# Three small token slots of a routed mixture of experts, moved from a split-weight path of their own into column tiles between the half layers of other experts

## The chip, the cores and the metric

The kernel runs on one core of one Trainium2 chip. The metric is the device time of one execution in microseconds (us); several runs are taken and their median is compared. Beside it there is one profiled execution, with a trace of every instruction on each engine: TensorE's matmuls (PE), its weight loads (PEld), VectorE (DVE), ScalarE (ACT), GpSimd (POOL) and SyncE (SP). The suffix q marks an engine's own queue work: DMA issues, register loads, waits.

## What is computed

A masked attention over 8 batches and 8 heads of 576 positions gives 4608 token rows of 512 numbers. Each row goes to the one of eight experts with the largest gate logit, through two matrix products with a ReLU between them, and is scaled by its gate weight:

```python
logits = x @ w_gate                       # (4608, 512) @ (512, 8)
expert_idx = np.argmax(logits, axis=1)
for e in range(8):
    mask = expert_idx == e
    h = np.maximum(x[mask] @ w1[e], 0.0)  # (512, 1024)
    out[mask] = gate_w[mask, None] * (h @ w2[e])  # (1024, 512)
```

The reference, run on its own inputs, sends 591, 497, 610, 490, 661, 437, 657 and 665 rows to experts 0 to 7.

## The kernel before

Attention and routing fill the first 240 us or so. The rest is the expert stage, with some expert work (`fillers`, then `base(0)`) already mixed into the end of the first part.

An expert's first 512 tokens are a base window (`base`, `window`, L255 to L306). Of experts 0, 2, 4 and 6 the first 256 are done early by `fillers`, so that their later windows have 256 tokens; those of 1, 3, 5 and 7 have 512. Tokens beyond 512 lie in slots of 128 (`slot`, L872). With the counts above that is 1, 0, 1, 0, 2, 0, 2 and 2 slots, eight in all, and `RSLOT = 8` of them are laid out statically. A loop at the end of the program, of `nslots - RSLOT` turns, takes what is beyond that number; here it has none.

Weights arrive in four chunks of 1 MB per expert (`wcat`; 80 such loads, issued by SP), each with a quarter of w1 and of w2. `wsplit` (L209) divides each chunk into a high part `whi` (ACT, L212) and a low part `wlo` (DVE, L213) in the fast fp32r format, and each product is taken as three matmuls: high by high, high by low, low by high. Raw and split weights have four buffers each in the expert stage.

A window goes by half layers: one chunk has two, a window eight. A half layer is twelve matmuls of w1 into bank `t` (L287 to L289), a ReLU on ACT (`hh`, L292), the low part on DVE (`hl`, L293), and then, one half layer late (`pend`), twelve (for 256 tokens six) matmuls of w2 (L276 to L278). A slot has four chunks of twelve matmuls of 256 columns (L892 to L894), two transposes (L904), and six matmuls of 512 columns (L911 to L913); four transposes of its tokens (L879) come first. Token rows are fetched by GpSimd (`gather`, L227) and written back by it (`finish`, L242).

The order is a list of jobs (L942): windows of experts 1 to 7 with one slot after each, and the last slot behind that: b1 s0 b2 s1 b3 s2 b4 s3 b5 s4 b6 s5 b7 s6 s7. While one job runs, the next one's gather and transposes are issued: gather before the first step, transposes at steps 0 and 2 (`PRE`). Base windows and slots share two PSUM banks named `v` for transposes. `slot_tables` (L654) computes, on DVE, which tokens lie in which slot, during the early windows.

A program orders the instructions of each engine by priority, which is program order except where the kernel raises it (`tc.high_priority`); an engine then works through its list in that order.

Of the kernel before, what the change touches and what calls it, by code (L numbers as in the profile page):

```python
# [7 lines left out]
F32 = mybir.dt.float32  # L8
# [27 lines left out]
RSLOT = 8  # L36
MAXSLOT = 40
XW = DM + 16
NCH = 4
CW = DF // NCH  # L40
CHW = 2 * 1024
LAG_T = 3
# [68 lines left out]
def host_constants(np):  # L111
    f = np.float32
    c = {}
    m = np.full((128, 3, 64), NEG, f)
    for p in range(128):
        q = p % QB
        m[p, 0, q + 1:q + QB + 1] = 0.0
        m[p, 1, max(q + 1, QB if p < 2 * QB else 0):q + QB + 1] = 0.0
        r, a = divmod(p % 64, SR)
        if r < 3:  # L120
            m[p, 2, r * SR:r * SR + a + 1] = 0.0
        else:
# [6 lines left out]
    parts = [tri, rows * np.arange(128, dtype=f),  # L129
             rows * np.arange(E, 0, -1, dtype=f), rows * np.arange(NT, dtype=f),  # L130
             np.arange(128, dtype=f).reshape(128, 1), np.arange(1, 129, dtype=f).reshape(128, 1)]
    c["blob"] = np.concatenate(parts, axis=1)
    return c
# [3 lines left out]
def moe_attn(ctx, tc, qk, vv, wg, wcat, blob0, blob, out):  # L137
# [29 lines left out]
    pid_sb = cst[:, 256 + E + NT:258 + E + NT]  # L167
    identb = const.tile([128, 128], BF16, name="identb")
# [4 lines left out]
    sidacc = const.tile([128, 2, MAXSLOT], F32, name="sidacc")  # L173
# [14 lines left out]
    srow = const.tile([128, MAXSLOT], I32, name="srow")  # L188
# [66 lines left out]
    def window(e, idc, odc, gpool, xpool, ypool, rows=N + 1):  # L255
# [4 lines left out]
        xh = xpool.tile([128, 4, n], F32R, name=f"xh{nt}")  # L260
        xl = xpool.tile([128, 4, n], F32R, name=f"xl{nt}")
# [42 lines left out]
    def base(e, gpool, xpool, ypool):  # L304
        tr = range(2 if e in EXP else 0, 4)
        return window(e, [ids[:, t, e:e + 1] for t in tr], [oids[:, t, e:e + 1] for t in tr], gpool, xpool, ypool)  # L306

    with ExitStack() as actx:
# [323 lines left out]
        def fillers():  # L632
            def make(e):
                w = window(e, [eids[:, t, e:e + 1] for t in range(2)], [eoids[:, t, e:e + 1] for t in range(2)], xge, xep, yep,
                           1 + EG * GT * 128)
                next(w)
                return w
# [15 lines left out]

        def slot_tables():  # L654
# [9 lines left out]
            cum = rte  # L664
            for sh in (1, 2, 4):
                nx = rt.tile([128, E], F32, name=f"cum{sh}")
                nc.vector.tensor_copy(out=nx[:, 0:sh], in_=cum[:, 0:sh])
                nc.vector.tensor_tensor(out=nx[:, sh:E], in0=cum[:, sh:E], in1=cum[:, 0:E - sh], op=ALU.add)
                cum = nx
# [7 lines left out]
            nc.vector.tensor_copy(out=srow, in_=es)  # L677
# [6 lines left out]
            nc.vector.tensor_tensor(out=oe, in0=oe, in1=first.unsqueeze(1).broadcast_to([128, NT, E]), op=ALU.mult)  # L684
            key = rt.tile([128, NT], F32, name="skey")
            nc.vector.tensor_reduce(out=key, in_=oe, axis=AX.X, op=ALU.add)
# [4 lines left out]
            nc.vector.scalar_tensor_tensor(out=key, in0=t1, scalar=1.0, in1=key, op0=ALU.is_ge, op1=ALU.mult)  # L691
            for g in range(NG):
# [5 lines left out]
                bm = scratch(GT * MAXSLOT).rearrange("p (t k) -> p t k", k=MAXSLOT)  # L698
                nc.vector.tensor_tensor(out=bm, in0=iota_sb[:, 1:MAXSLOT + 1].unsqueeze(1).broadcast_to([128, GT, MAXSLOT]),
                                        in1=key[:, gs].unsqueeze(2).broadcast_to([128, GT, MAXSLOT]), op=ALU.is_equal)  # L700
                bb = scratch(GT * MAXSLOT).bitcast(BF16).rearrange("p (t a k) -> p t a k", a=2, k=MAXSLOT)
                nc.vector.tensor_tensor(out=bb[:, :, 0, :], in0=bm, in1=tokhi_sb[:, gs].unsqueeze(2).broadcast_to([128, GT, MAXSLOT]),
# [4 lines left out]
                for c in range(GT):  # L707
                    nc.tensor.matmul(sb[:, 0:2 * MAXSLOT], am[:, c, :], bb[:, c, :, :].rearrange("p a k -> p (a k)"),
                                     start=(c == 0), stop=(c == GT - 1))
                acc = sidacc.rearrange("p a k -> p (a k)")  # L710
                nc.vector.tensor_tensor(out=acc, in0=sb[:, 0:2 * MAXSLOT], in1=acc, op=ALU.add)
            hi_ = rt.tile([128, MAXSLOT], F32, name="shi_")
            nc.vector.scalar_tensor_tensor(out=hi_, in0=sidacc[:, 0, :], scalar=128.0, in1=sidacc[:, 1, :], op0=ALU.mult, op1=ALU.add)
            nc.vector.tensor_copy(out=sids, in_=hi_)
            out_index(souts, hi_)
# [132 lines left out]
        with tc.high_priority():  # L848
            make_ids()
            cur = base(0, xge, xep, yep)  # L850
            next(cur)
# [75 lines left out]

    def row_load(in_tensor, engines):
# [12 lines left out]

    jobs = []  # L942
    for e in range(1, E):
        jobs.append(lambda e=e: base(e, xgm, xtm, yp))
        if e >= 1:
            jobs.append(lambda s=e - 1: static_slot(s))
    for s in range(E - 1, RSLOT):
        jobs.append(lambda s=s: static_slot(s))
# [135 lines left out]
```

## Time and profile before

| | us |
|---|---|
| median of three runs | 691.72 (690.84 to 693.19) |
| the profiled execution's own time | 688.08 |
| its span, first to last instruction | 686.2 |
| TensorE matmul busy | 648.9 (95% of the span) |
| TensorE weight load busy | 542.4 (79%) |
| VectorE busy | 431.2 (63%) |
| ScalarE busy | 354.5 (52%) |
| bytes moved | 149.85 MB, 218 GB/s over the span |

Matmuls are pipelined: a record's duration is its latency, and two neighbours overlap. What one costs in a dense stretch is the distance from its start to the next start, and that is read from the timeline. A stretch is one between two starts of the same kind of work.

### The profile page before, as it was taken

The numbers are of one execution on the slowest core, as the hardware profiler recorded it, in microseconds if no ns is written. First come the engines' busy times: TensorE is split into PE (matmuls) and PEld (weight loads), VectorE is DVE, ScalarE is ACT, GpSimd is POOL, SyncE is SP. The second block draws the span as 40 slices with busy tenths as digits, with TensorE's granted clock in tenths as the row PEclk, the third lists the DMA queues.
The fourth block names the chain that finished last, engine by engine and source line by source line (L and its number), as shares of the span: only waits on it lengthen the run. The fifth ranks groups of instructions, "written<-read, shape, count | busy, mean of one in ns | idle before, by whom it ended". The sixth has DMA issues, their size and how long they took to land.

```text
span 686.2 us, 14770 instructions
## 1 busy us (share of the span) xinstructions
PE 648.9 (95%) x5996; PEld 542.4 (79%) x5996; DVE 431.2 (63%) x796; ACT 354.5 (52%) x617; POOL 150.7 (22%) x168
## 2 busy tenths in 40 slices
PE   4999999799889899999999999999999999999997
PEld 3876768587778688897888988878888878988885
DVE  5667878567835579796336775346675248683364
ACT  1556666565555544564337574246473247572362
POOL 3222223511321302053005132022032041100021
PEclk9899999999999999999999999999999999999999
DMA  9879998985645657469327867337675257664140
GB/s 281 244 225 262 331 307 247 349 300 169 217 176 206 240 187 251 159 238 342 140 92 266 296 245 261 118 124 262 261 257 208 107 191 264 258 218 170 66 180 21
DMA packets 36695, 149.85 MB, mean 218 GB/s; under 512 B 5261, under 2 KB 5645, under 8 KB 26384
## 3 DMA queue, kind: packets, MB, share of 16 engines
q1 hardware_dynamic: 24576, 118.50, 51.1%
q0 software_dynamic: 6432, 20.26, 8.1%
q10 hardware_dynamic: 5616, 10.12, 4.1%
q8 instruction: 48, 0.79, 0.5%
q14 instruction: 23, 0.19, 0.1%
HBM read 129.69 MB, written 20.22 MB: 218 GB/s over the span
## 4 chain that ended last, share of the span: by engine, by line
PE 74%; issue 12%; DVE 5%; ACT 4%; DMA 2%; POOL 1%; POOLq 1%; SPq 0%; another core or an unknown queue 0%
PE t L287 8%; PE t L289 8%; PE t L288 8%; PE y L276 6%; PE y L278 6%; PE y L277 6%; PE s L399 4%; PE t L441 2%; PE s L412 2%; PE v L455 2%; PE v L466 2%; PE s L276 2%; PE s L278 2%; PE s L277 2%; PE v L265 2%
## 5 line engine op out<-in xcount | busy, mean ns | idle before, releaser
L213 DVE TENSOR_TENSOR wlo<-raw,whi 128x1024 fp32r<-128x1024 f32 x160 | 192.7, 1222 | 86.9 <-ACT whi L212 75.6
L212 ACT CAST whi<-raw 128x1024 fp32r<-128x1024 f32 x160 | 163.2, 1050 | 67.1 <-PE s L278 26.1
L287 PE MATMUL t<-xh,whi 128*128 128x256 f32 (+1 forms) x384 | 125.2, 327 | 1.9 <-ACT xh L221 1.3
L288 PE MATMUL t<-xl,whi 128*128 128x256 f32 (+1 forms) x384 | 123.8, 323 | 0.3 <-DVE xl L222 0.3
L289 PE MATMUL t<-xh,wlo 128*128 128x256 f32 (+1 forms) x384 | 123.4, 322 | 0.1
L292 ACT ACTIVATE hh<-t 128x256 fp32r<-128x256 f32 (+1 forms) x96 | 43.5, 453 | 115.1 <-PE t L289 109.2
L293 DVE SCALAR_TENSOR_TENSOR hl<-t,hh 128x256 fp32r<-128x256 f32 (+1 forms) x96 | 49.0, 510 | 75.6 <-ACT hh L292 75.2
L287 PEld LDWEIGHTS t<-xh,whi 128*128 128x128 f32 x384 | 72.4, 189 | 9.8 <-ACT xh L221 1.8
L288 PEld LDWEIGHTS t<-xl,whi 128*128 128x128 f32 x384 | 72.6, 189 | 7.2 <-DVE xl L222 0.7
L289 PEld LDWEIGHTS t<-xh,wlo 128*128 128x128 f32 x384 | 72.5, 189 | 6.4 <-DVE wlo L213 0.9
L276 PE MATMUL y<-whi,hh 128*128 128x512 f32 x192 | 76.2, 397 | 0.0
L277 PE MATMUL y<-wlo,hh 128*128 128x512 f32 x192 | 75.0, 391 | 0.0
L278 PE MATMUL y<-whi,hl 128*128 128x512 f32 x192 | 75.0, 396 | 0.0
L248 POOL DMA_INDIRECT out_dram<-y,oids x24 | 26.9, 1121 | 215.1 <-DVE y L247 166.5
L350 POOL TENSOR_TENSOR prob<-prob,ri 128x512 f32<-128x512 f32 x40 | 42.5, 1062 | 121.8 <-DVE ri L349 94.1
L155 ACT COPY xT<-v 128x270 f32<-128x270 f32 (+1 forms) x80 | 30.0, 481 | 29.0 <-PE v L455 13.0
L278 PEld LDWEIGHTS y<-whi,hl 128*128 128x128 f32 x192 | 35.6, 188 | 8.3
L276 PEld LDWEIGHTS y<-whi,hh 128*128 128x128 f32 x192 | 36.0, 188 | 6.7 <-ACT hh L292 0.7
L277 PEld LDWEIGHTS y<-wlo,hh 128*128 128x128 f32 x192 | 36.1, 188 | 5.7
L346 DVE TENSOR_REDUCE sm<-prob 128x8 f32<-128x512 f32 x40 | 27.3, 683 | 20.6 <-ACT prob L344 20.4
L340 DVE TENSOR_REDUCE nm<-s 128x8 f32<-128x512 f32 x40 | 27.3, 683 | 18.8 <-PE s L399 14.2
L344 ACT ACTIVATE prob<-prob 128x512 f32<-128x512 f32 x40 | 25.2, 631 | 22.9 <-DVE prob L343 22.1
(173 smaller groups left out, 1167.2 us busy)
## 6 DMA issues: line engine op xcount, KB each, us to landing
raw<-in_wcat_dram SPq DMA_DIRECT2D x80, 1024.0 KB, 6.5
xd<-xr ACTq DMA_DIRECT2D x36, 264.0 KB, 4.8
vl<-in_vv_dram SPq DMA_DIRECT2D x16, 512.0 KB, 6.5
qkl<-in_qk_dram SPq DMA_DIRECT2D x16, 264.0 KB, 3.8
vt<-in_vv_dram SPq DMA_DIRECT2D x16, 256.0 KB, 4.7
qk<-in_qk_dram SPq DMA_DIRECT2D x8, 484.0 KB, 5.5
qk<-in_qk_dram SPq DMA_DIRECT2D x8, 432.0 KB, 4.9
qk<-in_qk_dram SPq DMA_DIRECT2D x8, 396.0 KB, 6.3
```

Source lines behind the costliest of these rows:

```text
L155: nc.scalar.copy(out=out, in_=in_)
L212: nc.scalar.copy(out=hi[:, sl], in_=raw[:, sl])
L213: i = nc.vector.tensor_tensor(out=lo[:, sl], in0=raw[:, sl], in1=hi[:, sl].bitcast(F32), op=ALU.subtract)
L276: nc.tensor.matmul(yb[t], hh[:, ts], whi[:, w], start=(j == 0), stop=False)
L277: nc.tensor.matmul(yb[t], hh[:, ts], wlo[:, w], start=False, stop=False)
L278: nc.tensor.matmul(yb[t], hl[:, ts], whi[:, w], start=False, stop=(j == 7))
L287: nc.tensor.matmul(hb[:, 0:n], whi[:, w], xh[:, dc, :], start=(dc == 0), stop=False)
L288: nc.tensor.matmul(hb[:, 0:n], whi[:, w], xl[:, dc, :], start=False, stop=False)
L289: nc.tensor.matmul(hb[:, 0:n], wlo[:, w], xh[:, dc, :], start=False, stop=(dc == 3))
L292: nc.scalar.activation(out=hh[:, 0:n], in_=hb[:, 0:n], func=AF.Relu)
L293: nc.vector.scalar_tensor_tensor(out=hl[:, 0:n], in0=hb[:, 0:n], scalar=0.0, in1=hh[:, 0:n].bitcast(F32), op0=ALU.max, op1=ALU.subtract)
L350: lastp[0] = nc.gpsimd.tensor_tensor(out=pv, in0=pv, in1=ri.unsqueeze(2).broadcast_to([128, 8, 64]), op=ALU.mult)
```

## The change

`RSLOT` goes from 8 to 5, and up to `NSM = 3` slots that would hold at most 32 tokens (`SMT`) leave the slot list. `slot_tables` marks the experts whose last slot has so few, ranks them, takes their slots out of the count, and gives their tokens table columns of their own; `ident[:, 0:32]` in four column tiles copies the 32 token numbers to all four groups of partitions. With the counts above, experts 4, 6 and 7 have such a slot, with 21, 17 and 25 tokens, and five slots of the old kind are left.

A small slot (`small`) loads its weights unsplit through ACT's DMA queue, two chunks at a time into two buffers. It multiplies in plain fp32: a step of `mm1` is 4 chunks of depth by 4 column tiles of 32 columns each, 16 matmuls with 32 stationary and 128 moving columns; `mm2` has the same shape. Two halves `p` of two chunks each make a slot. The steps are issued at marked ticks (`SIDE`) inside the windows of experts 3, 5 and 7: a window has a tick after the w1 matmuls of each half layer and one after the w2 matmuls behind them. All steps of a small slot share one `v` bank. The first weight load of the next small slot is at tick 14.

The jobs become b1 s0 b2 s1 w3 s2 b4 w5 s3 b6 w7 s4, where w is a window with ticks. Two windows now follow a window (b4 to w5, b6 to w7). `xh` and `xl` are one pair of buffers for both window sizes, and `xgm` has 8 buffers, not 9.

```diff
-RSLOT = 8
+RSLOT = 5
 MAXSLOT = 40
+NSM = 3
+SMT = 32
+TCOL = MAXSLOT + NSM
...
+ORDER = (("b", 1), ("s", 0), ("b", 2), ("s", 1), ("w", 3), ("s", 2), ("b", 4), ("w", 5), ("s", 3), ("b", 6), ("w", 7), ("s", 4))
+SIDE = (0, 2, 3, 4, 5, 6, 11, 12, 13)
+SIDE_NEXT = 14
...
-        xh = xpool.tile([128, 4, n], F32R, name=f"xh{nt}")
-        xl = xpool.tile([128, 4, n], F32R, name=f"xl{nt}")
+        xh = xpool.tile([128, 4, xw], F32R, name="xh")[:, :, 0:n]
+        xl = xpool.tile([128, 4, xw], F32R, name="xl")[:, :, 0:n]
...
                 pend.append((hh, hl, whi, wlo, fl, j))
+                tick()
                 if len(pend) > 1:
                     mm2(*pend.pop(0))
+                tick()
                 yield
...
+            last = rt.tile([128, E], F32, name="last")
+            nc.vector.scalar_tensor_tensor(out=last, in0=rte, scalar=-128.0, in1=rem, op0=ALU.mult, op1=ALU.add)
+            few = rt.tile([128, E], F32, name="few")
+            nc.vector.tensor_scalar(out=few, in0=last, scalar1=float(SMT - 128), scalar2=None, op0=ALU.is_le)
+            rank = rt.tile([128, E], F32, name="rank")
+            nc.vector.tensor_tensor(out=rank, in0=running(few, "rank"), in1=few, op=ALU.subtract)
+            nc.vector.scalar_tensor_tensor(out=few, in0=rank, scalar=float(NSM), in1=few, op0=ALU.is_lt, op1=ALU.mult)
+            nc.vector.tensor_tensor(out=rte, in0=rte, in1=few, op=ALU.subtract)
+            cum = running(rte, "cum")
...
+            key = of_expert(first, "skey")
+            yield
+            whole = of_expert(rte, "whole")
+            small_key = of_expert(rank, "smkey")
             yield
...
+            for i in range(128 // SMT):
+                nc.tensor.matmul(rp[SMT * i:SMT * i + SMT, 0:NSM], ident[:, 0:SMT], hi_[:, MAXSLOT:TCOL],
+                                 start=True, stop=True, tile_position=(0, SMT * i))
...
-    xgm = ctx.enter_context(tc.tile_pool(name="xgm", bufs=9))
+    xgm = ctx.enter_context(tc.tile_pool(name="xgm", bufs=8))
...
+    smp = ctx.enter_context(tc.tile_pool(name="smp", bufs=1))
...
+    def small(s):
+
+        row = row_load(srow[0:1, MAXSLOT + s:MAXSLOT + s + 1], [mybir.EngineType.Activation])
+
+        def load(p):
+            w = [smp.tile([128, CHW], F32, name="sraw", bufs=2) for _ in range(2)]
+            for i in range(2):
+                nc.scalar.dma_start(out=w[i], in_=wcat[bass.ds(row + (2 * p + i) * 128, 128), :])
+            return w
+
+        w = load(0)
+        yield
+        xg = gather(smp, smid[:, s:s + 1])
+        yield
+        vb = bank("v")
+        for dc in range(4):
+            nc.tensor.transpose(vb[:, dc * 128:(dc + 1) * 128], xg[:, dc * 128:(dc + 1) * 128], ident)
+        xt = smp.tile([128, 4, SMT], F32, name="sxt")
+        nc.scalar.copy(out=xt, in_=vb.rearrange("p (c k) -> p c k", c=4)[:, :, 0:SMT])
+        yield
+        for p in range(2):
+            for dc in range(4):
+                for i in range(4):
+                    c0 = dc * CW + (i % 2) * 128
+                    nc.tensor.matmul(vb[SMT * i:SMT * i + SMT, 128:256], xt[:, dc, :], w[i // 2][:, c0:c0 + 128],
+                                     start=(dc == 0), stop=(dc == 3), tile_position=(0, SMT * i))
+            hs = smp.tile([128, 128], F32, name="shr")
+            nc.scalar.activation(out=hs, in_=vb[:, 128:256], func=AF.Relu)
+            yield
+            nc.tensor.transpose(vb[:, 256:384], hs, ident)
+            ht = smp.tile([128, 128], F32, name="sht")
+            nc.scalar.copy(out=ht, in_=vb[:, 256:384])
+            yield
+            for f in range(4):
+                for i in range(4):
+                    c0 = 1024 + (f % 2) * 512 + 128 * i
+                    nc.tensor.matmul(vb[SMT * i:SMT * i + SMT, 0:128], ht[:, SMT * f:SMT * f + SMT], w[f // 2][:, c0:c0 + 128],
+                                     start=(f == 0), stop=(f == 3), tile_position=(0, SMT * i))
+            if p == 0:
+                y0 = smp.tile([128, 128], F32, name="sy0")
+                nc.scalar.activation(out=y0, in_=vb[:, 0:128], func=AF.Copy, scale=xg[:, DM:DM + 1])
+                yield
+                w = load(1)
+                yield
...
+    def tick():
+        if side and clock[0] in SIDE:
+            next(side[0], None)
+        if side and clock[0] == SIDE_NEXT and smalls:
+            next(smalls[0])
+        clock[0] += 1
...
     for i in range(len(jobs)):
         nxt = None
+        if ORDER[i][0] == "w":
+            side.append(smalls.pop(0))
+            clock[0] = 0
...
+        if ORDER[i][0] == "w":
+            drain_(side.pop())
+        elif i == 0:
+            next(smalls[0])
```

## Rows read from the trace of the kernel before

**Rows 1.** The page, its first two parts: busy time of each engine, and, of the span in 40 slices, the clock that TensorE was granted.

```profile
PE 648.9 (95%) x5996; PEld 542.4 (79%) x5996; DVE 431.2 (63%) x796; ACT 354.5 (52%) x617; POOL 150.7 (22%) x168
PEclk9899999999999999999999999999999999999999
```

**Rows 2.** The expert stage cut at the starts of the slots, one row for each stretch: its length, busy time of each engine with instruction counts, granted clock, share of the DMA engines and GB/s. A stretch of 36 to 39 us is a slot and a window of 256 tokens, one of 59.7 a slot and a window of 512, the last one two slots.

```profile
361.90:398.00 36.10, 36.10 (x236) 32.49 (x235) 25.68 (x35) 22.95 (x38) 11.00 (x10) 1.00 0.77 275
457.70:496.60 38.90, 36.20 (x235) 32.31 (x234) 25.73 (x35) 23.16 (x38) 9.32 (x10) 1.00 0.69 256
556.30:595.30 39.00, 36.33 (x235) 32.45 (x234) 25.77 (x35) 23.16 (x38) 9.38 (x10) 1.00 0.71 253
398.00:457.70 59.70, 59.63 (x296) 49.27 (x295) 31.18 (x38) 26.47 (x39) 10.20 (x7) 1.00 0.53 185
496.60:556.30 59.70, 59.70 (x295) 49.35 (x294) 31.20 (x38) 26.46 (x39) 10.14 (x7) 1.00 0.52 182
595.30:655.00 59.70, 59.70 (x295) 49.36 (x295) 31.23 (x38) 26.46 (x39) 5.17 (x4) 1.00 0.47 168
655.00:681.50 26.50, 25.85 (x165) 21.58 (x163) 16.53 (x22) 16.23 (x28) 4.79 (x5) 1.00 0.25 90
```

**Rows 3.** What TensorE's matmuls waited for from 300 us to the end: in total, times, longest.

```profile
PE v L904 <- DVE xl L222: 2.5, 2, 1.3
PE v L904 <- ACT hr L897: 1.3, 1, 1.3
PE v L904 <- DVE wlo L213: 1.3, 1, 1.3
```

**Rows 4.** TensorE's timeline in a slot and the window after it: start in us, latency, line, operation, shape, count.

```profile
458.01 0.28 PE L892 MATMUL t<-whi,sxh 128*128 128x256 f32 x1
458.13 0.28 PE L893 MATMUL t<-wlo,sxh 128*128 128x256 f32 x1
...
459.07 0.60 PE L265 MATMUL v<-cst,xg 128*128 128x128 f32 x4
459.43 0.36 PE L892 MATMUL t<-whi,sxh 128*128 128x256 f32 x1
459.63 0.28 PE L893 MATMUL t<-wlo,sxh 128*128 128x256 f32 x1
...
465.18 0.39 PE L911 MATMUL s<-whi,shh 128*128 128x512 f32 x1
465.41 0.40 PE L912 MATMUL s<-wlo,shh 128*128 128x512 f32 x1
```

**Rows 5.** TensorE's timeline around one call of the gate's matmuls, which lie in four column tiles of 32 columns as those of the change do: L516 has four matmuls in plain fp32, two records each, with 384 moving columns.

```profile
231.24 0.39 PE L278 MATMUL y<-whi,hl 128*128 128x512 f32 x1
231.56 0.85 PE L516 MATMUL v<-xT,wg_sb 128*32 128x384 f32 x8
232.34 0.55 PE L523 MATMUL v<-cst,ls 128*128 128x128 f32 x3
```

**Rows 6.** TensorE's timeline in the attention stage: scores with 16-strided stationary columns in two column tiles (L399), and the products with the values, stationary columns side by side, in two column tiles too (L466); both in plain fp32 with 64 moving columns.

```profile
104.07 2.05 PE L399 MATMUL s<-qkl 128*64 128x64 f32 x32
105.95 2.03 PE L466 MATMUL v<-pTl,vl 128*64 128x64 f32 x64
107.92 0.66 PE L508 MATMUL y<-cst,xT 128*128 128x128 f32 x4
```

**Rows 7.** Weight loads of these three lines (L399 and L466 of rows 6, L516 of rows 5), grouped by form: busy us in total, mean ns of one.

```profile
L399 PEld LDWEIGHTS s<-qkl 128*64 128x64 f32 x512 | 31.0, 210 | 7.2 <-issue 6.6 <-DMA qk<-in_qk_dram 0.6
L466 PEld LDWEIGHTS v<-pTl,vl 128*64 128x64 f32 x512 | 16.3, 138 | 2.3 <-issue 2.1
L516 PEld LDWEIGHTS v<-xT,wg_sb 128*32 128x32 f32 x48 | 1.2, 108 | 3.5 <-ACT xT L155 2.6 <-issue 0.9
```

**Rows 8.** Two pieces of 10 us of the stretch in which `slot_tables` runs (columns as in rows 2); three neighbouring operations on VectorE with few numbers, in order of start; and one of the tables' operations with 288 numbers, grouped (busy us, mean ns).

```profile
250.00:260.00 10.00, 9.94 (x73) 8.69 (x72) 9.89 (x26) 3.94 (x6) 0.00 (x0) 1.00 0.38 120
...
270.00:280.00 10.00, 10.00 (x66) 8.94 (x65) 9.13 (x17) 3.55 (x6) 0.00 (x0) 1.00 0.44 139
...
253.72 0.17 DVE L668 TENSOR_TENSOR cum<-cum 128x6 f32<-128x6 f32 x1
253.79 0.18 DVE L689 TENSOR_SCALAR t<-tfall 128x36 f32<-128x36 f32 x1
253.88 0.18 DVE L619 CAST ids<-hi__4179 128x32 int32<-128x32 f32 x1
...
L684 DVE TENSOR_TENSOR prob<-prob,first 128x288 f32<-128x288 f32 x1 | 0.5, 454 | 0.0
```

**Rows 9.** TensorE's timeline where a window follows a window before the change (`base(0)`, then expert 1).

```profile
314.57 0.82 PE L265 MATMUL v<-cst,xg 128*128 128x128 f32 x6
316.03 0.70 PE L287 MATMUL t<-xh,whi 128*128 128x512 f32 x2 [0.64 <-issue]
```

**Rows 10.** Loads of a raw weight chunk of 1 MB from 316 us on, from issue to landing; SP's register load of a slot's expert and its DMA issues (ns, min/median/max); and GpSimd's gather for a slot, a whole job ahead of its transposes.

```profile
DMA to landing us min/median/max: 4.9/6.5/10.1
...
L929 SPq TENSOR_LOAD <-srow x8: 262/265/276, 309.6 to 619.7; - x8
L938 SPq DMA_DIRECT2D raw<-in_wcat_dram x32: 332/333/352, 313.6 to 659.3; - x32
...
405.43 0.97 POOL L229 DMA_INDIRECT xg<-xd,sids  x1 [0.30 <-issue]
```

More of the change, by code (lines that the diff above doesn't have):

```diff
@@ L172, in moe_attn @@
     eall = const.tile([128, NT], F32, name="eall")
-    sidacc = const.tile([128, 2, MAXSLOT], F32, name="sidacc")
+    sidacc = const.tile([128, 2, TCOL], F32, name="sidacc")
     nc.vector.memset(sidacc, 0.0)
@@ L187, in moe_attn @@
     souts = const.tile([128, MAXSLOT], I32, name="souts")
-    srow = const.tile([128, MAXSLOT], I32, name="srow")
+    srow = const.tile([128, TCOL], I32, name="srow")
+    smid = const.tile([128, NSM], I32, name="smid")
+    smout = const.tile([128, NSM], I32, name="smout")
     nsl = const.tile([128, 1], I32, name="nsl")
@@ L253, in finish, with window @@
         lastp[0] = i
-    def window(e, idc, odc, gpool, xpool, ypool, rows=N + 1):
+    def window(e, idc, odc, gpool, xpool, ypool, rows=N + 1, tick=lambda: None, xw=BASE):
         nt = len(idc)
@@ L302, in window, with base @@
         yield
-    def base(e, gpool, xpool, ypool):
+    def base(e, gpool, xpool, ypool, **kw):
         tr = range(2 if e in EXP else 0, 4)
-        return window(e, [ids[:, t, e:e + 1] for t in tr], [oids[:, t, e:e + 1] for t in tr], gpool, xpool, ypool)
+        return window(e, [ids[:, t, e:e + 1] for t in tr], [oids[:, t, e:e + 1] for t in tr], gpool, xpool, ypool, **kw)
     with ExitStack() as actx:
@@ L652, in scratch, with running @@
             return probs.tile([128, 512], F32, name="prob")[:, 0:n]
+        def running(v, name):
+            for sh in (1, 2, 4):
+                nx = rt.tile([128, E], F32, name=f"{name}{sh}")
+                nc.vector.tensor_copy(out=nx[:, 0:sh], in_=v[:, 0:sh])
+                nc.vector.tensor_tensor(out=nx[:, sh:E], in0=v[:, sh:E], in1=v[:, 0:E - sh], op=ALU.add)
+                v = nx
+            return v
         def slot_tables():
@@ L676, in slot_tables @@
             nc.vector.tensor_scalar(out=es, in0=es, scalar1=float(E - 1), scalar2=float(NCH * 128), op0=ALU.min, op1=ALU.mult)
-            nc.vector.tensor_copy(out=srow, in_=es)
+            nc.vector.tensor_copy(out=srow[:, 0:MAXSLOT], in_=es)
+            nc.vector.tensor_tensor(out=few, in0=few, in1=iota_sb[:, 0:E], op=ALU.mult)
+            fe = scratch(NSM * E).rearrange("p (k e) -> p k e", e=E)
+            nc.vector.tensor_tensor(out=fe, in0=iota_sb[:, 0:NSM].unsqueeze(2).broadcast_to([128, NSM, E]),
+                                    in1=rank.unsqueeze(1).broadcast_to([128, NSM, E]), op=ALU.is_equal)
+            nc.vector.tensor_tensor(out=fe, in0=fe, in1=few.unsqueeze(1).broadcast_to([128, NSM, E]), op=ALU.mult)
+            fs = rt.tile([128, NSM], F32, name="fs")
+            nc.vector.tensor_reduce(out=fs, in_=fe, axis=AX.X, op=ALU.add)
+            nc.vector.tensor_scalar(out=fs, in0=fs, scalar1=float(NCH * 128), scalar2=None, op0=ALU.mult)
+            nc.vector.tensor_copy(out=srow[:, MAXSLOT:TCOL], in_=fs)
+            nc.vector.tensor_scalar(out=rank, in0=rank, scalar1=float(MAXSLOT + 1), scalar2=None, op0=ALU.add)
             yield
@@ L691, in slot_tables @@
             nc.vector.scalar_tensor_tensor(out=key, in0=t1, scalar=1.0, in1=key, op0=ALU.is_ge, op1=ALU.mult)
+            nc.vector.tensor_tensor(out=whole, in0=t1, in1=whole, op=ALU.is_gt)
+            nc.vector.tensor_tensor(out=small_key, in0=small_key, in1=key, op=ALU.subtract)
+            nc.vector.tensor_tensor(out=small_key, in0=small_key, in1=whole, op=ALU.mult)
+            nc.vector.tensor_tensor(out=key, in0=key, in1=small_key, op=ALU.add)
             for g in range(NG):
@@ L849, in moe_attn @@
             make_ids()
-            cur = base(0, xge, xep, yep)
+            cur = base(0, xge, xep, yep, xw=BASE // 2)
             next(cur)
@@ L926, in moe_attn, with drain_ @@
     SP = mybir.EngineType.SP
+    def drain_(gen):
+        for _ in gen:
+            pass
     def row_load(in_tensor, engines):
@@ L940, in static_slot @@
         return slot(sids[:, s:s + 1], souts[:, s:s + 1], load)
-    jobs = []
[L943 to L948, printed above, removed]
+    out4 = out.rearrange("n (i d) -> (n i) d", i=4)
+    def small(s):
[39 more added lines that the diff above has]
+                yield
+        y = smp.tile([128, 128], F32, name="sy")
+        nc.vector.scalar_tensor_tensor(out=y, in0=vb[:, 0:128], scalar=xg[:, DM:DM + 1], in1=y0, op0=ALU.mult, op1=ALU.add)
+        i = nc.gpsimd.indirect_dma_start(out=out4, out_offset=bass.IndirectOffsetOnAxis(ap=smout[:, s:s + 1], axis=0), in_=y,
+                                         in_offset=None, bounds_check=4 * N - 1, oob_is_err=False)
+        unordered(i, "out")
+        yield
@@ new lines, in moe_attn @@
+    side = []
+    clock = [0]
+    def tick():
[4 more added lines that the diff above has]
+        clock[0] += 1
+    jobs = []
+    for kind, n in ORDER:
+        if kind == "b":
+            jobs.append(lambda e=n: base(e, xgm, xtm, yp))
+        elif kind == "w":
+            jobs.append(lambda e=n: base(e, xgm, xtm, yp, tick=tick))
+        else:
+            jobs.append(lambda s=n: static_slot(s))
@@ L949, in moe_attn @@
+    smalls = [small(s) for s in range(NSM)]
     cur = jobs[0]()
```

49 lines of the change are left out of this document (28 added, 21 removed).

## The prediction

> **What bounds the kernel now.** I read the page first: TensorE is busy 95% of the span, and its clock is at the upper of its two levels (2.4 GHz) for at least nine tenths of every slice but the second [rows 1]. Busy time counts latencies that overlap, so it says little alone. Hence the cut of the expert stage at the starts of the slots [rows 2]: in each stretch VectorE and ScalarE have over a quarter of their time free, and the DMA engines are at 0.47 to 0.77, falling to 0.25 at the end. Last the waits: from 300 us on TensorE's matmuls waited for VectorE or ScalarE in four places, some 5 us in all [rows 3]. So there the length is TensorE's own work, and an instruction less on it is time less. The exception is two of the three stretches of a slot and a 256 window: 38.9 and 39.0 us against 36.1, 2.8 us of stall each, where transposes wait for VectorE [rows 2, 3].
>
> **What is removed.** Three slots of 128. The last stretch holds two slots in 26.5 us: 13.2 us each [rows 2]. By count: 48 matmuls of 256 columns at 0.12 us from start to start, and 24 of 512 at 0.23, are 11.3 us; four token transposes cost 0.44 (459.07 to 459.63 without the one matmul between) [rows 4]; the other 1.5 us are eight transposes of `hr` and their turns. Both ways agree, so a 512 window is 59.7 - 13.2 = 46.5 us. All three lie on the path: 3 x 13.2 = 39.6 us. Their splits (ScalarE and VectorE) vanish too, off the path, and worth nothing as long as TensorE is the bound.
>
> **What is added on TensorE.** The trace has no matmul of just this form. The nearest is the gate's [rows 5]: plain fp32, four column tiles of 32, four matmuls in eight records. From its start to the next work it takes 0.78 us. Each tile streams 2 x 384 = 768 columns; a step of the small slot streams 4 x 2 x 128 = 1024 columns for each tile, so 0.78 x 1024 / 768 = 1.04 us. Getting in costs 0.32 instead of 0.23 us between starts: 0.09 more. A step is 1.13 us. It has 32 records, though, not eight, so I check the rate of records: L466, two column tiles with adjacent stationary columns, does 64 in 1.97 us, 31 ns each, which is 0.98 us for 32, still below. L399, with strided stationary columns and weight loads of 210 ns, needs 59 ns each [rows 6, 7]: 1.9 us a step. The small slot's stationary columns are adjacent and 32 wide, as L516's, whose loads take 108 ns [rows 7]; I take the first value. Bounds: 1.0 us, and 32 x 107 = 3.4 us if the tiles ran one after another (107 ns is a third of the 0.32 that a gate record has in the 0.64 us left of 0.78 without a turn of 0.14; an estimate). A small slot is four steps, four token transposes (0.44) and two single ones (under 0.3 each): 4 x 1.13 + 0.44 + 0.6 = 5.6 us, three are 16.7. That the steps are spread over half layers matters: ReLU, copy and transpose between two steps have a 12-matmul block of 2.8 us to hide in.
>
> One rule of the Trainium skill speaks against that price. TensorE: Matmul & The Clock Gate, section "Wait — 56ns, not 53.3ns?", says that with hardware decoding off the sequencer needs about 62 ns for each matmul, which binds where the array's work is shorter. By it a step would be 2.0 us and the sum 10 us worse. The trace has both: L399 at 59 ns, L466 at 31 [rows 6], so here it is not a general limit.
>
> **What is added elsewhere.** (1) Tables on VectorE: some 27 operations with few numbers at about 0.08 us from start to start, and four more with 288 numbers of at most 0.45 us: 4 us, in a stretch where VectorE is busy 0.91 to 0.99 [rows 8]. TensorE is about full there too, so only a part reaches it: bounds 0 and 4, I take 1.5. (2) ACT's queue: a small slot issues four weight loads and one register load; by SP's rows 0.33 and 0.27 us each [rows 10], so a load of a half is under 1 us. Behind it on ScalarE stand the next `hh` and `whi`; `hh` has a block of 2.8 us before its w2 matmuls need it, and ScalarE is busy 26.5 of 59.7 us [rows 2]. The second half's load waits on ScalarE until TensorE has read the first half's weights, hence the queue stands still there for a moment. Bounds 0 and 1.9 us for a slot, I take 0.5: 1.5 in all. (3) Two joints where a window follows a window. The one before the change has an idle time of 0.64 us [rows 9]: 1.3 us; bounds 0 and 4. The y banks are no worse than at that joint. (4) GpSimd gets a gather and a scatter for each small slot. Gathers are issued as soon as a buffer is free, a job ahead [rows 10], and with one more user the small slot's should be too: nothing; without that cover TensorE would stand at the four token transposes until the rows have landed. Behind a scatter that waits for `y` stand only gathers that are as early. (5) The shared `v` bank leaves one for the next slot's transposes, whose first use is over before it is needed again: nothing. (6) Bytes: the same weights, 12 of the MB now through ACT's queue and inside the wide stretches, which are the thinly loaded ones (168 to 185 GB/s against 253 to 275 in the narrow ones [rows 2]); SP's queue has 12 loads less. Nothing, with the second half's load as the exception (rival C). One `xh` pair and 8 `xgm` buffers suffice for two jobs in flight: nothing.
>
> **The sum.** -39.6 + 16.7 + 1.5 + 1.5 + 1.3 = -18.6 us. Against the profiled execution's 688.08 this gives 669.5; the median of the runs shown is 691.72, 3.6 higher, and there it gives 673.1. The two stalls of 2.8 us (s2 to b4, and the one at b6) keep their surroundings in the new order, so I leave them; they may vanish (-5.6), which with (1) to (3) at nothing is 663. With (1) to (3) at their upper ends it is 673.1 + 2.5 + 4.1 + 2.7 = 682.4.
>
> **Rivals.**
> A. Records bind at 59 ns, as at L399: each step 1.9 + 0.09 = 2.0 instead of 1.13 us, twelve steps, +10.3: 683.4. For it: 32 short records in a row; against: L466 at 31 ns.
> B. The column tiles don't overlap, so that a step is 3.5 us: 12 x 2.4 = +28.4, 701.5, slower than before. It lies in the `mm1` and `mm2` steps alone, and it decides once a step exceeds 2.7 us ((39.6 - 4.3 - 3.1) / 12). Against: the gate's eight records in 0.78 us [rows 5], which in turn would be 2.56. For: the change has 128 columns in a record, so that loads come three times as often, and 32 loads of 108 ns in turn would be the same 3.5 us.
> The Trainium skill, TensorE: Matmul & The Clock Gate, section "Part 3: Packing small matmuls — row/col tiling", says that a weight load runs beside matmuls in flight only where the row groups differ; four column tiles share all rows, so by it B holds. Rows 5 has the same sharing and doesn't show it.
> C. The second half's weights come late. They are issued after tick 5 and used at tick 11, six blocks of 12 matmuls at 0.23 later: 16.6 us. One chunk lands in 6.5 us, at worst 10.1 [rows 10]; two, one behind the other, 13.0 or 20.2. At worst TensorE stands for 3.6 us three times: +10.8, 683.9.
> D. The marks find other small slots than 21, 17 and 25 tokens (or none), and the slots go to the loop at the end, where nothing overlaps: at least the 39.6 us back, over 691.7. The counts come from the reference itself, so this is unlikely.
>
> **How the numbers follow.** Forecast 0.66, A 0.10, C 0.09, B 0.05, D 0.02; 0.08 for what I don't see, half of it still faster. The time is the forecast's, 673. The range runs from 663, all small costs at nothing, to 684, which takes in A and C; outside are B, D and most of the rest. A difference of 0.3%, about 2 us, is what a measurement of this kernel can tell from no change. Faster by more: 0.66 + 0.10 + 0.09 + 0.04 = 0.89; within: 0.03; slower: B, D and a little, 0.08.
>
> **What would show it right or wrong.** The new matmul lines with 128*32 by 128x128: 32 records from first to last start in about 1.0 us, 2.0 for A, 3.5 for B. The wide stretch from the first matmul of s1 to that of s2 should be 59.7 + 5.6 + 0.5 us; from the first of s2 to that of s3 (b4 and w5 between) 38.9 + 46.5 + 5.6 + 1.2 = 92.2. In C the first records of the second half's `mm1` wait for a DMA into `sraw`. Waits of `hh` or `whi` behind ACT's DMA issues would show (2) dearer; a later first slot, (1). It is wrong if TensorE's free time in the stage grows by more than 5 us, since then the removed work was not the bound.

## The result and the profile after

The changed kernel takes 672.81 us in the median (668.48 to 675.88, four runs), the kernel before 691.82 (690.84 to 693.19). The ratio is 0.9719, 95% interval 0.9657 to 0.9781: 19.0 us less, where 18.6 less were forecast. The profiled execution took 671.04 us, its span is 668.8. The page, busy time of each engine [rows 1]:

```profile
PE 626.7 (94%) x6136; PEld 522.0 (78%) x6154; DVE 400.9 (60%) x788; ACT 327.3 (49%) x584; POOL 148.1 (22%) x168
```

TensorE is still busy nearly throughout. Where the time went is read from the expert stage, cut as in [rows 2]; the first row runs from the first matmul of b1 to that of s0, the last from that of s4 to the end:

```profile
320.18:368.59 48.41, 46.04 (x205) 37.00 (x205) 18.91 (x23) 15.30 (x21) 3.38 (x4) 1.00 0.54 208
368.59:410.13 41.54, 38.40 (x236) 34.02 (x234) 25.90 (x35) 23.10 (x38) 9.38 (x10) 0.96 0.66 239
410.13:474.92 64.79, 64.79 (x429) 52.88 (x428) 30.47 (x38) 27.96 (x45) 12.12 (x9) 1.00 0.65 223
474.92:562.84 87.92, 87.92 (x580) 74.09 (x579) 45.52 (x59) 40.44 (x66) 18.39 (x17) 1.00 0.67 238
562.84:650.71 87.87, 87.87 (x580) 74.11 (x578) 46.63 (x60) 40.39 (x66) 15.23 (x13) 1.00 0.49 176
650.71:663.50 12.79, 12.78 (x81) 10.47 (x79) 4.32 (x7) 5.41 (x11) 3.08 (x4) 1.00 0.21 82
```

From s1 to the end it is 253.4 us (410.13 to 663.50) against 283.5 (398.00 to 681.50 in [rows 2]): 30.1 less. Ahead of s1, 12.1 were lost: b1 starts 4.2 later than in [rows 9], its stretch is 48.4 instead of 45.9 (316.03 to 361.90), and that of s0 is 41.5 instead of 36.1. Of these 12.1, the 5.4 in the stretch of s0 are in no other traced execution (experiment 1), and the start of b1 differs by 5 us from one execution to another (experiment 4).

A step of a small slot, from TensorE's timeline; the first row is the last w2 matmul before it, the third the first w1 matmul behind it:

```profile
434.08 0.39 PE L288 MATMUL s<-whi,hl 128*128 128x512 f32 x1
434.40 1.08 PE L1031 MATMUL v<-sraw,sxt 128*32 128x128 f32 x32
435.41 0.50 PE L297 MATMUL t<-xh,whi 128*128 128x512 f32 x1
```

The 32 records take 1.01 us from their first start to the start of the next work, and getting in takes 0.32 us between starts, as at the gate [rows 5]. What matmuls waited for from 300 us on (before: [rows 3]):

```profile
PE y L286 <- ACT hh L302: 2.1, 1, 2.1
PE v L963 <- ACT hr L956: 1.4, 1, 1.4
PE v L963 <- DVE xl L232: 1.0, 1, 1.0
PE t L297 <- ACT xh L231: 0.8, 2, 0.6
PE t L299 <- DVE wlo L223: 0.5, 1, 0.5
PE s L970 <- ACT shh L231: 0.2, 1, 0.2
```

No matmul waits for `sraw`. The top row is new: in b1, the w2 matmuls of L286 stand still until `hh` is there. ScalarE's timeline says why (ACTq is its queue work):

```profile
322.99 1.06 ACT L231 CAST xh<-v 128x512 fp32r<-128x512 f32 x2
329.28 0.36 ACTq L1014 DMA_DIRECT2D sraw<-in_wcat_dram  x1
329.68 0.60 ACT L302 ACTIVATE hh<-t 128x512 fp32r<-128x512 f32 x1 [5.64 <-DMA out_dram<-y,oids]
```

The first small slot's weight load stands in ScalarE's order in front of b1's first `hh`. It waits for DMAs that write token rows out, and ScalarE is idle for 5.64 us behind the wait.

### The profile page after: what moved, and what is told of

Its sections match the earlier page's. It is cut to its first block, busy times and chain, and to the rows that moved or that the text cites. A ratio compares the mean times of both kernels' runs of the same rounds, so it can differ in the third digit from the quotient of the medians.

```text
span 668.8 us, 14979 instructions
## 1 busy us (share of the span) xinstructions
PE 626.7 (94%) x6136; PEld 522.0 (78%) x6154; DVE 400.9 (60%) x788; ACT 327.3 (49%) x584; POOL 148.1 (22%) x168
## 4 chain that ended last, share of the span: by engine, by line
PE 35%; issue 34%; POOL 7%; DMA 5%; DVE 4%; ACT 2%; POOLq 1%; ACTq 0%; another core or an unknown queue 0%
POOL xg L239 4%; PE t L297 4%; PE t L299 4%; PE t L298 4%; PE y L286 4%; PE y L287 3%; PE y L288 3%; POOL out_dram L258 2%; PE s L411 2%; DMA raw<-in_wcat_dram 1%; PE v L520 1%; DMA out_dram<-y,oids 1%; PE v L467 1%; DMA xg<-xd,eids 1%; DMA xd<-xr 1%
## 5 line engine op out<-in xcount | busy, mean ns | idle before, releaser
L223 DVE TENSOR_TENSOR wlo<-raw,whi 128x1024 fp32r<-128x1024 f32 x136 | 164.0, 1222 | 76.2 <-ACT whi L222 68.1
L222 ACT CAST whi<-raw 128x1024 fp32r<-128x1024 f32 x136 | 139.3, 1051 | 63.4 <-PE s L288 25.4
L297 PE MATMUL t<-xh,whi 128*128 128x256 f32 (+1 forms) x384 | 126.9, 332 | 2.3 <-ACT xh L231 2.1
L286 PE MATMUL y<-whi,hh 128*128 128x512 f32 x192 | 77.2, 402 | 2.1 <-ACT hh L302 2.1
L162 ACT COPY xT<-v 128x270 f32<-128x270 f32 (+1 forms) x80 | 30.1, 480 | 28.8 <-PE v L467 12.3
L286 PEld LDWEIGHTS y<-whi,hh 128*128 128x128 f32 x192 | 36.4, 189 | 9.4 <-ACT hh L302 2.9
L239 POOL DMA_INDIRECT xg<-xd,ids x24 | 30.2, 1259 | 31.9 <-ACT xh L231 18.9
```

What stands on the lines that cost most here:

```text
L222: nc.scalar.copy(out=hi[:, sl], in_=raw[:, sl])
L223: i = nc.vector.tensor_tensor(out=lo[:, sl], in0=raw[:, sl], in1=hi[:, sl].bitcast(F32), op=ALU.subtract)
L239: lastp[0] = nc.gpsimd.indirect_dma_start(out=xg, out_offset=None, in_=xd[0:rows, :], in_offset=bass.IndirectOffsetOnAxis(ap=idc, axis=0))
L286: nc.tensor.matmul(yb[t], hh[:, ts], whi[:, w], start=(j == 0), stop=False)
```

## The experiments

The theory: TensorE's own work sets the length, a small step costs about 1.1 us of it, and what was mis-sized is the first load on ScalarE's queue. The rivals are that the gain is from the new order of the jobs or from the buffers, that the price of a step is a rate of records that would grow with them, and that ScalarE's queue is the wrong place for the loads. The kernel before took 691.8 us in the first comparison and 681.1 to 681.5 in the later ones; so across comparisons only ratios, stretches and the distance to the kernel before are compared.

**1. The changed kernel again, and with its first load behind b1's last `hh`.** Each was run in two comparisons.

```diff
-                nc.scalar.activation(out=hh[:, 0:n], in_=hb[:, 0:n], func=AF.Relu)
+                acts[0] = nc.scalar.activation(out=hh[:, 0:n], in_=hb[:, 0:n], func=AF.Relu)
...
-                nc.scalar.dma_start(out=w[i], in_=wcat[...])
+                d = nc.scalar.dma_start(out=w[i], in_=wcat[...])
+                if s == 0 and p == 0:
+                    issue_after(d, acts[0])
```

> The changed kernel with one edit: the first small slot's two weight loads stand on ACT's queue behind the last hh of b1. In the changed kernel they stand in front of b1's first hh and wait for the scatters of the early windows, and ScalarE was idle for 5.6 us there. Theory 1 (that wait in ACT's queue is what b1 lost): from b1's first matmul to s0's first 45.9 us instead of 48.4, as in the kernel before, and the total 2.5 us shorter. Rival (b1 lost the time to the transfer itself, or another instruction takes the wait over): b1 stays at 48.4, total unchanged. The stall and the low clock in s0 and b2 (41.5 us against 36.1) should go if they came from this load, and stay if they did not.

> The changed kernel once more, unedited, beside the others, because its four times spread over 668.5 to 675.9 us with granted clocks of 0.988 to 0.981. Theory 1 (the loss in b1 stands in the instruction order): b1 takes 48.4 us again. Theory 2 (the 36.1 to 41.5 us of s0 and b2 is a stall that comes and goes with small shifts of time, and drags the clock down with it): that stretch may come out anywhere between 36 and 41.5. Rival to 2 (it belongs to the order of the instructions): 41.5 again. Total 672.8, by theory 2 within 668 to 676.

> The kernel with the first small load behind b1's last hh, once more. In the profiled executions b1 took 45.4 us with this edit, against 48.4 and 51.6 without it, but the medians of the two were 660.6 and 661.2. Theory (the wait stands in every execution): 3 to 6 us below the changed kernel run beside it. Rival (the scatters land later in some executions than in others, and the wait is mostly short): medians within 1.5 us of each other, and profiles that differ.

> The changed kernel beside the run before. Theory (wait in every execution): b1 takes 48 to 52 us, total 3 to 6 us above the run with the edit. Rival: total within 1.5 us of it.

| | median us | ratio to before (95%) |
|---|---|---|
| changed kernel, second time | 661.19 | 0.9706 (0.9671 to 0.9740) |
| with the edit | 660.59 | 0.9703 (0.9661 to 0.9745) |
| changed kernel, third time | 666.87 | 0.9788 (0.9748 to 0.9829) |
| with the edit again | 660.30 | 0.9684 (0.9647 to 0.9720) |

The changed kernel the second time: the stretches of b1 and of s0, and between them pieces of 5 us in b1:

```profile
317.53:369.10 51.57, 48.24 (x204) 39.08 (x205) 18.91 (x23) 15.18 (x21) 3.36 (x4) 0.93 0.52 194
325.00:330.00 5.00, 1.70 (x4) 1.42 (x5) 1.72 (x3) 1.57 (x3) 0.98 (x1) 0.70 1.01 407
330.00:335.00 5.00, 5.00 (x15) 3.93 (x15) 0.16 (x1) 0.00 (x0) 0.00 (x0) 0.62 0.95 392
335.00:340.00 5.00, 5.00 (x24) 4.14 (x23) 0.69 (x1) 1.22 (x2) 0.00 (x0) 1.00 0.04 18
369.10:405.25 36.15, 36.15 (x236) 32.63 (x234) 25.64 (x35) 22.99 (x38) 9.75 (x10) 1.00 0.76 274
```

ScalarE was idle for 6.81 us there, and L286 waited 3.3. During the wait TensorE does next to nothing, and behind it the granted clock is at the lower level (1.2 GHz; 0.50 in each microsecond from 328 to 333) until about 334 us; hence 15 matmul records in one piece and 24 in the next, and a b1 stretch of 51.6 us. The wait was 2.4 us the third time and 2.1 in the first profile; there the clock stayed at 2.4 GHz in b1, which took 49.7 and 48.4 us. The third time, b1:

```profile
318.32:368.00 49.68, 46.12 (x204) 37.04 (x205) 18.89 (x23) 15.26 (x21) 3.38 (x4) 1.00 0.56 204
```

With the edit (the b1 stretches of its two runs, and between them, from the first, ScalarE's first `hh` of b1 and the load):

```profile
318.16:363.57 45.41, 45.41 (x204) 37.24 (x205) 19.00 (x23) 15.28 (x21) 3.38 (x4) 1.00 0.50 182
```

```profile
324.07 0.60 ACT L303 ACTIVATE hh<-t 128x512 fp32r<-128x512 f32 x1 [2.60 <-PE t L300]
...
359.18 0.88 ACTq L1015 DMA_DIRECT2D sraw<-in_wcat_dram  x2
```

```profile
318.12:364.40 46.28, 45.73 (x205) 37.15 (x205) 19.00 (x23) 15.38 (x21) 3.37 (x4) 1.00 0.49 178
```

The load now stands behind b1's last `hh`. The first `hh` follows its own matmuls, and b1 takes 45.4 and 46.3 us, 6.2 and 3.4 less than in the changed kernel's trace of the same comparison. In total time the means of six runs differ by 1.1 us in one comparison (662.18 and 661.05) and by 6.4 in the other (666.65 and 660.29); over both it is 3.7. In the comparison with 1.1, the traced execution of the changed kernel (666.49 us) is the slowest of its six, and the other five (660.43 to 663.30) lie among those with the edit (657.39 to 664.63). So the traces show that the load holds b1 up; in total time one comparison of two shows it, and how much it costs in a usual execution stays open. The stall in s0 (41.5 us at a clock of 0.96 in the first profile) is absent in both repeats (36.1 and 36.2), so it comes and goes with the execution. The version with the edit has the lowest ratio of all complete kernels here.

**2. No small steps at all.** The rows of the three small slots are left out.

```diff
-    smalls = [small(s) for s in range(NSM)]
+    smalls = []
...
-            side.append(smalls.pop(0))
...
-            drain_(side.pop())
-        elif i == 0:
-            next(smalls[0])
```

> The changed kernel without any step of the small slots: no loads, no matmuls, no scatters of theirs, so that 63 rows of the output stay unwritten. The tables and the order of jobs stay. Theory (a small slot costs 5.6 us of TensorE plus 0.5 of waits, and the first load's wait 2.5 us): 672.8 - 18.2 - 2.5 = 652; the stretch from s1 to s2 59.7 us, from s2 to s3 82.8. Rival (the steps cost far less, because they fill gaps): 660 or more. Rival (the loads disturb the transfers of the others): below 648.

It took 643.77 us, ratio 0.9456 (0.9405 to 0.9507). Its stretches s1 to s2 and s2 to s3:

```profile
397.59:456.61 59.02, 59.02 (x296) 49.43 (x294) 31.06 (x38) 26.49 (x39) 10.15 (x7) 1.00 0.53 186
456.61:538.72 82.11, 82.11 (x446) 70.62 (x445) 44.97 (x58) 38.92 (x60) 15.13 (x15) 1.00 0.55 199
```

So a small slot costs 64.79 - 59.02 = 5.77 and 87.92 - 82.11 = 5.81 us of TensorE's path with everything that it brings, three cost 17.4. In total time this kernel is 37.4 us below the kernel before (681.12), and the version with the later first load is 20.9 and 20.8 below the kernel before of its own comparisons; the difference is 16.5.

**3. The price of a step.** In one run each of its 16 matmuls is done twice (the second pass starts the sums anew, other than the expectation says; only work is added). In another the same matmuls are done with one column tile finished before the next begins. The first, shown for `mm1`, and likewise in `mm2`:

```diff
-            for dc in range(4):
+            for dc in (0, 1, 2, 3) * 2:
                 for i in range(4):
```

> The changed kernel with the matmuls of each of the twelve steps issued twice, which adds them twice into the same sums: hidden rows and outputs of the small slots are scaled wrongly, nothing else. 32 more records for each step. Theory (a record costs TensorE 27 to 32 ns in a dense run of four tiles): 0.85 to 1.04 us a step, 10 to 12.5 us in all, 3.4 to 4.2 in the stretch from s1 to s2. Rival A (59 ns a record): 22.7 us. Rival (steps lie in idle time): near 0.

For the other, the two loops change places in `mm1` and `mm2`:

```diff
-            for dc in range(4):
-                for i in range(4):
+            for i in range(4):
+                for dc in range(4):
```

> The changed kernel with the two loops of each step exchanged: all matmuls of one column tile, then those of the next. The same products and sums. Theory (the four tiles run side by side only because neighbours in the queue go to different tiles, and starts keep the order of the queue): a step goes from about 1 to 3.2 or 3.5 us, twelve steps, 26 to 29 us more, so 699 to 702. Rival (the tiles overlap in any order): 672.8.

Twice: 675.46 us, ratio 0.9905 (0.9871 to 0.9940). Its stretch s1 to s2, and a doubled step in the timeline:

```profile
401.30:469.56 68.26, 68.26 (x557) 56.39 (x556) 31.50 (x39) 27.77 (x45) 12.11 (x9) 1.00 0.61 219
```

```profile
433.25 1.95 PE L1043 MATMUL v<-sraw,sht 128*32 128x128 f32 x64
435.14 0.50 PE L297 MATMUL t<-xh,whi 128*128 128x512 f32 x1
```

128 records more cost 68.26 - 64.79 = 3.47 us: 27 ns each, 0.87 for 32. Tile after tile: 681.74 us, ratio 0.9979 (0.9944 to 1.0013):

```profile
406.11:476.40 70.29, 70.29 (x430) 58.41 (x428) 31.59 (x39) 27.86 (x45) 12.84 (x9) 1.00 0.59 212
```

```profile
438.57 2.46 PE L1043 MATMUL v<-sraw,sht 128*32 128x128 f32 x32
440.96 0.50 PE L297 MATMUL t<-xh,whi 128*128 128x512 f32 x1
```

The same 32 records now take 2.39 us from start to next start, 75 ns each, and a slot 70.29 - 64.79 = 5.5 us more. That is less than the 107 ns estimated for tiles that don't overlap at all, so the size in the expectation was wrong. Its direction holds: here neighbours in different column tiles overlap far more than neighbours in the same one, and the order of the two loops decides whether the change is worth anything.

**4. What else the change brings, alone.** The order of the jobs, in the kernel before; then the new kernel's tables and buffers with the old order and all eight slots:

```diff
+    for kind, n in [(x[0], int(x[1])) for x in "b1 s0 b2 s1 b3 s2 b4 b5 s3 b6 b7 s4 s5 s6 s7".split()]:
...
```

> The kernel before with its jobs in the order b1 s0 b2 s1 b3 s2 b4 b5 s3 b6 b7 s4 s5 s6 s7: the order of the change, with the three slots behind at the end. Theory (the two joints of window to window cost nothing, and a slot with a 256 window between two wide ones is where the 2.8 us stalls arose): s2 to s3, with b4 and b5, 82.8 us; three of them would be 5.6 us faster than before, less what the last four slots in a row cost, whose splits on VectorE are about as long as their matmuls: 0 to 1 us each; 686 to 691. Rival (the stalls come and go with time shifts): they turn up anywhere, and the total is 691.8 give or take 3. Rival (a joint costs 0.65 us, as the one at the end of the early windows): 1.3 us more.

```diff
-RSLOT = 5
+RSLOT = 8
...
-scalar1=float(SMT - 128)
+scalar1=-128.0
...
-    smalls = [small(s) for s in range(NSM)]
+    smalls = []
```

> The changed kernel with the mark set so that no slot counts as small: eight full slots in the order of before, but with the longer tables, the shared xh and xl, and 8 xgm buffers. What is computed stays the same. Theory (the prediction's price for the tables): 1.5 us over the kernel before, bounds 0 and 4, all of it ahead of b1, so 693.3. Rival (the tables cost the whole 4 us that b1 came later in the changed kernel): 696. Another (nothing, as TensorE is full there): 691.8. From s0 on the stretches should be as before: 36, 60, 39, 60, 39, 60 and 26.5 us; if a buffer that was taken away matters, one of them grows.

Order: 679.92 us, ratio 0.9975 (0.9953 to 0.9998), so at most a small part of the gain. Tables: 681.19, ratio 0.9998 (0.9970 to 1.0026). Order's stretches s0 to s1, s1 to s2 and s2 to s3 (two windows side by side in the last) and its last four slots, which follow one another; then two stretches of the tables' kernel:

```profile
360.40:396.44 36.04, 36.04 (x235) 32.41 (x234) 25.60 (x35) 22.97 (x38) 11.00 (x10) 1.00 0.76 275
396.44:456.16 59.72, 59.65 (x296) 49.30 (x294) 31.20 (x38) 26.50 (x39) 10.17 (x7) 1.00 0.53 185
456.16:538.78 82.62, 82.62 (x446) 70.37 (x444) 45.09 (x58) 38.97 (x60) 15.13 (x15) 1.00 0.55 198
621.44:673.40 51.96, 51.80 (x333) 44.29 (x331) 40.30 (x50) 37.98 (x62) 8.24 (x7) 1.00 0.60 214
```

```profile
458.11:494.26 36.15, 36.15 (x236) 32.65 (x234) 25.62 (x35) 22.97 (x38) 9.77 (x10) 1.00 0.77 276
494.26:553.26 59.00, 59.00 (x295) 49.46 (x294) 31.06 (x38) 26.48 (x39) 10.16 (x7) 1.00 0.52 185
```

Three things follow. A slot of 128 is worth 13.0 us: 51.96 / 4 in the four slots in a row, and 36.15 + 59.00 - 82.11 between the tables' kernel and that of experiment 2. A joint of two windows costs nothing: with the slot of the first reading, in which no joint of windows lies, the stretch should take 36.04 + 59.72 - 13.0 = 82.8 us, and 82.62 was measured. And the stalls of 2.8 us in [rows 2] are in neither kernel, nor in the two of experiment 6, though all but the first of these keep the old order: they come and go. The tables' price can't be told from the front of the stage: b1 starts between 314.2 and 319.3 us in the four traced kernels without them (mean 316.6) and between 314.5 and 320.2 in the ten with them (mean 317.5).

**5. The loads on SP's queue instead of ScalarE's.**

```diff
-[mybir.EngineType.Activation]
+[SP]
...
-                nc.scalar.dma_start(out=w[i], in_=wcat[...])
+                nc.sync.dma_start(out=w[i], in_=wcat[...])
```

> The changed kernel with the small slots' weight loads and register loads on SP's queue. Theory 1 (waits in ACT's queue cost TensorE time): b1 takes 45.9 instead of 48.4 us, total 2.5 us shorter, unless SP's own raw loads are held up behind the wait for the first half's weights; then a wide window after a tick 6 shows waits for raw or whi, up to some us each. Rival (the queue doesn't matter): total and stretches as in the changed kernel, 672.8.

It took 675.00 us, ratio 0.9912 (0.9880 to 0.9944), 13.8 us more than the changed kernel beside it. The stretches s1 to s2, s2 to s3 and s3 to s4, then SP's queue's longest wait from 400 to 660 us, and TensorE's there:

```profile
398.66:468.02 69.36, 65.37 (x433) 53.22 (x431) 25.65 (x36) 24.16 (x44) 15.50 (x13) 1.00 0.41 148
468.02:562.01 93.99, 90.05 (x578) 75.14 (x578) 45.61 (x59) 40.58 (x67) 16.93 (x16) 0.98 0.56 219
562.01:653.65 91.64, 90.33 (x574) 75.76 (x575) 51.47 (x62) 43.89 (x68) 13.84 (x10) 0.97 0.55 219
```

```profile
SPq L1014 <- PE v L1043: 120.6, 5, 28.8
```

```profile
PE t L951 <- ACT whi L222: 6.6, 2, 4.0
```

A load into a buffer that TensorE still reads waits at the head of SP's queue, up to 28.8 us, and the raw chunks of the next window stand behind it. The wide stretches lose 4.6, 6.1 and 3.8 us against the first profile, some 9 of them in waits; in the last two the granted clock is lower too (0.98 and 0.97). b1 takes 45.4 us here, as with the edit of experiment 1. So ScalarE's queue is the better place, except for the first load.

**6. Why the matmuls of 512 columns come closer together.** A 512 window and a slot take 59.0 us in the kernels of 2 and of the tables, and 59.7 in the kernel before. Two differences, alone in the kernel before: one `xh` pair for both window sizes, and constants whose widths move what lies behind them.

```diff
-        xh = xpool.tile([128, 4, n], F32R, name=f"xh{nt}")
+        xh = xpool.tile([128, 4, xw], F32R, name="xh")[:, :, 0:n]
```

> The kernel before with one part of the change: one pair of xh and xl buffers for both window sizes. In the runs with all of the change's buffers, dense matmuls of 512 columns start 0.2267 us apart on the mean, in the kernel before and with its order changed 0.2303, which is 0.6 to 0.7 us for a 512 window with its 192 of them. Theory 1 (where the tiles lie in memory sets that distance, and the shared pair moves them): a slot and a 512 window take 59.0 us instead of 59.7. Rival (it is the widened constants): 59.7. In total 0 to 3 us either way.

```diff
+    pad1 = const.tile([128, 1], F32, name="pad1")
...
+    pad2 = const.tile([128, 6], F32, name="pad2")
```

> The kernel before with nothing but small unused tiles between its constants, of the sizes by which the change widens them, so that all later tiles lie where those widths put them. Theory (the address of the tiles, moved by the widths): a slot and a 512 window take 59.0 us instead of 59.7, and matmuls of 512 columns start 0.2267 us apart. Rival (the shared pair of xh): 59.7 and 0.2303. In total 0 to 3 us either way.

They took 679.90 us, ratio 0.9982 (0.9953 to 1.0010), and 680.46, ratio 0.9990 (0.9964 to 1.0017); their stretches s1 to s2 are 59.72 and 59.71 us. Neither is the cause by itself. The two together, and eight `xgm` buffers instead of nine with what that moves, weren't tried.

## Why the prediction was right, point by point

- **The bound.** TensorE's own work: taking the small steps away moved the total by 16.5 us for 17.4 in the stretches (2); doing their products twice left 5.7 of the 20.3 or 14.2 us that the two repeats gained, so 14.6 or 8.5 went, for 3 x 3.47 = 10.4 in the stretches (3).
- **Three slots removed:** 3 x 13.0 = 39.1 us, predicted 39.6.
- **Small steps:** 1.01 + 0.09 = 1.10 us, predicted 1.13; a small slot 5.8 with its share of ScalarE's queue, predicted 5.6 + 0.5. The columns of the gate gave the right size. The 1.01 is to be set against the 1.04, as both hold the turn to the next work. The records alone are 0.87 (3), where the prediction's 0.64 for the gate without its turn scales to 0.64 x 1024 / 768 = 0.85. The rest, 0.14, is what the prediction took for the turn at the gate, there without a row; whether the turn is what it consists of was not measured by itself.
- **Rival A** is out: 27 ns for a record, not 59. The 62 ns for each matmul that the Trainium skill states for hardware decoding off (TensorE: Matmul & The Clock Gate, "Wait — 56ns, not 53.3ns?") don't bind here either: 27 ns for a record, and 54 for each of the program's matmuls of two records, are both below it. Whether hardware decoding was on, no run here shows.
- **Rival B,** tiles that don't overlap, is out: 1.01 us, not 3.5. The Trainium skill's rule behind it (same page, "Part 3: Packing small matmuls — row/col tiling") doesn't describe these records, whose tiles share all rows: a step's 32 weight loads of 110 ns each, 3.5 us in turn, lie within 0.81 us (row below). The prediction also read more into the section than it says: the same section of the Trainium skill has a table with a speedup of 2.38 for three column tiles of 512 columns, which no run here has, so B does not follow from the section as a whole. The rival's break-even of 2.7 us for a step is roughly borne out by experiment 3: at 2.39 + 0.09 the kernel is back at the time of the one before.

```profile
434.40 0.81 PEld L1031 LDWEIGHTS v<-sraw,sxt 128*32 128x32 f32 x32 [0.35 <-issue]
```

- **Rival C** is out: no wait for `sraw`. **D** is out: L951 has 80 matmuls, 16 for each of five static slots, and the loop has no turn.
- **Tables:** predicted 1.5 between 0 and 4; measured 0.9 later at b1 within a scatter of 5 us. Neither shown nor refuted.
- **ACT's queue, the term that failed.** The prediction spread 1.5 us evenly over the slots, because `hh` has a block of 2.8 us in reserve. That holds for the loads inside the windows. For the first load it doesn't: it waits for the write-backs of the early windows, and the wait, 5.6 to 6.8 us, exceeds the reserve. This one load costs b1 2.5 to 6.2 us in the traces, and 1.1 and 6.4 us in the mean total time of the two comparisons. The kernel before had such a wait on ScalarE there too, but behind b1's first `hh`, where no matmul waited for it:

```profile
326.21 0.59 ACT L221 CAST sxh<-v 128x512 fp32r<-128x512 f32 x1 [3.73 <-DMA out_dram<-y,oids]
```

- **Joints,** predicted 1.3: 0. The 0.64 of [rows 9] stands only there, behind `base(0)`, not between two windows of the new order.
- **Stalls kept,** 5.6 us in the base: they are gone in the new order, but also in kernels with the old one. Leaving them in the base took an accident of one execution for a property. The kernel before was not traced again in the later comparisons, where it took 681 us, so whether the stalls are a part of those 10 us isn't shown.

So the total was right because misses cancel, and that is luck. In the first profile the stage from s1 on gained 30.1 us where 39.6 - 16.7 - 1.5 - 1.3 = 20.1 were forecast. The 10.0 more are the stalls (5.6), the joints (1.3), the closer matmuls (0.7 in each of three windows) and small remainders. Ahead of s1 the same profile lost 12.1 where 1.5 were forecast, and the first load is only 2.5 of that: 5.4 are the stall in s0, and 4.2 the later start of b1, of which no run shows how much is the tables. In the two repeats the gain was 20.3 and 14.2 us, so the 18.6 lie within what the comparisons themselves differ by. The two stretches named ahead show the misses on the one side: s1 to s2 took 64.8 us instead of 65.8, and s2 to s3 87.9 instead of 92.2, where a stall of 2.8 us didn't come, the joint and the step's price were about 1.0 smaller (6.8 and 5.8), and the closer matmuls gave 0.7.

## What to carry to other kernels

Small remainders were cheap here in plain fp32 column tiles between dense blocks, as long as neighbouring matmuls went to different tiles. A DMA issue on a compute engine's queue stands in that engine's order, as the 5.64 us of ScalarE show: ask what its buffer was used for last, and put the first issue behind the work that others wait for. Stalls of one profile that have no stated cause don't belong in the base of a sum.

## What was not expected of the hardware

- 32 records of 128 columns in four column tiles: 27 ns each in turns of tiles, 75 ns tile by tile.
- With a wait of 3.3 us in b1, in which TensorE had next to nothing to do, the granted clock fell to 1.2 GHz for 3 to 7 us, in the changed kernel's second run and in both kernels of experiment 3; with waits of 2.1 and 2.4 us there it did not. The length of one wait doesn't settle it: in s0 of the first profile the clock fell to that level (0.50 from 384 to 386 us) behind two waits of 0.5 and 1.1 us close together.
- In the 512 windows, matmuls of 512 columns start every 0.2267 us in the changed kernel and every 0.2303 in the one before, with the same clock and the same instructions; 0.7 us in a window. In both fences below, the second row is the ninth start after the first (the rows between are left out); first the kernel before, then the changed one. The cause stays open (experiment 6).

```profile
342.60 0.40 PE L287 MATMUL t<-xh,whi 128*128 128x512 f32 x1
...
344.67 0.39 PE L287 MATMUL t<-xh,whi 128*128 128x512 f32 x1
```

```profile
333.23 0.39 PE L297 MATMUL t<-xh,whi 128*128 128x512 f32 x1
...
335.27 0.39 PE L297 MATMUL t<-xh,whi 128*128 128x512 f32 x1
```
